# Second raw buffer, later transposes and gated GpSimd work in a fused attention and wave-MLP kernel

## The chip, the cores and the metric

The kernel runs on one core of one Trainium2 chip. Times are device microseconds (us) of one execution. Executions are called fast or slow by their time and their granted TensorE clock (the share of TensorE's full speed that the chip allowed); only fast ones enter a ratio. A difference counts as slower or faster only from 2% on; where a smaller one is called slower, its 95% interval leaves out 1.

## The reference

Windowed attention with four sink positions feeds a "wave" MLP. The cut version:

```python
# q, k, v: (4 batches, 8 heads, 768, 64); n_sink 4, window 128
scores = scale * q @ k^T
keep   = (column < 4) | (0 <= row - column < 128)
a      = softmax(where(keep, scores, -1e9))
x      = (a @ v)                      # heads side by side: (4, 768, 512)
theta  = x @ w_theta
y      = w_tok_r @ (x * cos(theta)) + w_tok_i @ (x * sin(theta))
u      = x + y
out    = u + relu(u @ w_ch)           # float32
```

## The kernel before

Heads are worked on in pairs: four pairs a batch, sixteen "slots" (0 to 15). A slot holds a pair's scores, its exponentials (ScalarE), the mask products (VectorE) and the values of the pair before (slots 11 and 15 do the mask products of two pairs), and a token block of the previous batch's MLP: 12 token-mixing matmuls (`yp`, in four "pieces"), the sum `u`, its transpose `uT`, and four channel matmuls (`wp`). The transposed q and k of pairs 0 to 11 are copied into place by ScalarE or VectorE; those of the last batch (12 to 15) are transposed by DMA straight into the form that the scores read. Pairs 10 and 11 go through a "raw" buffer and a copy. A tile pool with n buffers makes the writer of the n+1st tile wait for the readers of the first.

The program keeps its own order on TensorE, ScalarE, GpSimd and SP from the start, and on VectorE from batch 1 on. So where a line stands in a slot decides what it queues behind.

```python
    vstage = pool("vstage", 4)      # float32 v as loaded
    cast = pool("cast", 2)          # q, k as bf16
    qkt = pool("qkt", 3)            # q, k transposed
    qkr = pool("qkr", 1)            # raw transposes of pairs 10 and 11
    ...
    def pool_copy(out, in_):
        nc.gpsimd.tensor_scalar(out=out, in0=in_, scalar1=1.0, scalar2=1.0, op0=ALU.mult, op1=ALU.mult)

    QK_DMA = range(12, NPAIR)
    QK_RAW = (10, 11)
    V_CAST = range(12, NPAIR)       # v loaded and cast by GpSimd's own DMA

    def load_cast_v(i):
        ...
        nc.gpsimd.dma_start(out=vx[:, :, 0:D], in_=v[b, 2 * hp:2 * hp + 2].rearrange("h (t p) d -> p (h t) d", p=P))

    def transposed_by_dma(i):
        if i in QK_RAW:
            for name in ("q", "k"):
                raw = qkr.tile([P, NT, P], BF16, name=f"{name}r", tag=f"{name}r")
                nc.sync.dma_start_transpose(out=raw, in_=qk_c.pop((name, i))...)
        if i not in QK_DMA:
            return
        for name in ("q", "k"):
            ...
            nc.sync.dma_start_transpose(out=x..., in_=c...)

    def mask_product(i, c):
        E, r = e_t[i], (slice(0, 1024), slice(1024, NE))[c - 1]
        nc.vector.tensor_tensor(out=E[:, :, r], in0=E[:, :, r], in1=mask2[:, :, r], op=ALU.mult)

    def mix(b, t, lo, hi):          # one piece: three of the twelve yp matmuls
        ...
        if hi == 2 * NT:
            ...                     # u = yp + x on VectorE
            if (b, t) not in U_PE:
                nc.sync.dma_start_transpose(out=uT, in_=u)

    def sink_values(b):             # four GpSimd copies
        for tb in range(NB):
            nc.gpsimd.tensor_scalar(out=vsinks[b % 2][:, tb, :, 0:D], in0=vsf[:, b - 2, :, :], ...)

    def slot(i, blk, wtok=None):
        ...
        if i + 2 < HP or HP <= i < NPAIR - 2:
            cast_qk(i + 2)          # GpSimd
        cast_v(i)
        if i + 2 in V_CAST:
            load_cast_v(i + 2)
        ...                         # scores, pieces
        if not first:
            mask_product(i - 1, 1)
            mask_product(i - 1, 2)
        transposed_by_dma(i + 2)
        ...
        if not first:
            piece(blk, 3)           # u and its transpose
        if hp > 0:
            weigh(i - 1, 0)         # values of the pair before
            weigh(i - 1, 1)
        ...
        finish()                    # wp

    # main loop, batches 1 to 3
            if b > 1:
                slot(i, (p, hp))
                if b == 2 and hp == 3:
                    sink_values(3)
    ...
        phases(b, 2)                # the last cos and sin (cs) and products z of the batch
```

The softmax here doesn't subtract the row's maximum and nothing guards it: scores larger than these inputs give would overflow.

## Time and profile before

| kernel before | value |
|---|---|
| median, runs | 183.4 us, 3 runs, 182.77 to 183.54 |
| span of the profiled execution | 180.9 us (device time 182.63 us) |
| mean granted TensorE clock | 0.999 |
| TensorE busy | 169.5 us, 94% |

The lines that carry the argument are shown in the prediction. TensorE is the bound, and its waits are short: 1.6 us from 84 to 145 us. A line of the waits reads "engine, operation and line, <- engine and tile waited for: us in total, times, longest". A line of an engine in order of time reads "start, duration, engine, line, operation, output<-input, count", with the idle time ahead of it in brackets.

One more view is needed for comparison: the mask products "of slots 9 and 11" on VectorE, in the kernel before. Those of slot 9 are pair 9's, which the program does in slot 10; the four of slot 11 are those of pairs 10 and 11.

```profile
91.27 3.00 DVE L247 TENSOR_TENSOR E<-E,mask 128x2048 bf16<-128x2048 bf16 x2
97.38 5.05 DVE L247 TENSOR_TENSOR E<-E,mask 128x2048 bf16<-128x2048 bf16 x4
```

### The profile page before, as it was taken

To read this page: it belongs to the slowest core of one execution; us is meant where nothing else is said; L and a number is where in the kernel's file an instruction comes from. 1 tells how busy PE (TensorE), PEld (TensorE's weight loads), DVE (VectorE), ACT (ScalarE), POOL (GpSimd) and SP (SyncE) were. 2 spreads that over 40 slices of the span, in tenths; PEclk is the share of its full clock that TensorE was granted. 3 is DMA by queue.
4 is the path that set the end of the run, shared out by engine and by line. 5 is a ranking of instruction groups with operands and counts; after the bars stand their busy time and mean duration, and the time that the engine had idled before them with its cause. 6 is when DMAs were issued, how large, how long until landed. Compare 5 with 4: busy or idle time off the path is not lost.

```text
span 180.9 us, 4035 instructions
## 1 busy us (share of the span) xinstructions
PE 169.5 (94%) x1619; PEld 88.4 (49%) x1619; DVE 121.9 (67%) x215; ACT 105.7 (58%) x112; POOL 75.4 (42%) x101
## 2 busy tenths in 40 slices
PE   7799998999999989999998899989999999999991
PEld 2345664554565656443553454434555544344550
DVE  6477867892866688386698981885978816824451
ACT  4897869629768486699998503797454039200000
POOL 8996689987764805038098300750000000000000
PEclk9999999999999999999999999999999999999999
DMA  5999999999998997991399956999733520133413
GB/s 176 307 312 266 350 381 410 383 349 332 328 300 264 287 297 183 282 207 32 102 136 192 220 144 170 297 139 176 118 94 98 147 70 2 59 106 97 145 60 116
DMA packets 73106, 36.80 MB, mean 203 GB/s; under 512 B 61184, under 2 KB 67584, under 8 KB 73088
## 3 DMA queue, kind: packets, MB, share of 16 engines
q1 hardware_dynamic: 65584, 35.60, 71.1%
q0 software_dynamic: 7360, 0.82, 7.3%
q8 instruction: 12, 0.20, 0.5%
q10 hardware_dynamic: 144, 0.13, 0.2%
q14 instruction: 6, 0.05, 0.1%
HBM read 25.82 MB, written 6.29 MB: 178 GB/s over the span
## 4 chain that ended last, share of the span: by engine, by line
PE 64%; ACT 15%; DVE 11%; DMA 3%; issue 3%; POOL 2%; DVEq 0%; ACTq 0%; POOLq 0%
PE yp L372 24%; PE wp L400 9%; PE thp L330 9%; PE avp L277 5%; PE sc L228 5%; ACT E L241 3%; DVE zz L343 3%; ACT cs L339 3%; DVE E L247 3%; ACT cs L340 3%; DMA uT<-u 3%; PE sc L221 2%; PE tp L202 2%; PE wtp L357 2%; PE xtp L307 2%
## 5 line engine op out<-in xcount | busy, mean ns | idle before, releaser
L372 PE MATMUL yp<-zz,wrT 128*128 128x512 bf16 x138 | 52.4, 380 | 1.6 <-DVE zz L343 1.2
L241 ACT ACTIVATE E<-sc 128x1024 bf16<-128x1024 f32 x48 | 47.6, 1032 | 10.6 <-PE sc L228 8.7
L372 PE MATMUL yp<-zz,wiT 128*128 128x512 bf16 x138 | 52.3, 379 | 0.6 <-DVE wiT L361 0.3
L343 DVE TENSOR_TENSOR zz<-cs,x_nat 128x1024 bf16<-128x1024 bf16 x24 | 21.6, 936 | 14.3 <-ACT cs L340 14.3
L247 DVE TENSOR_TENSOR E<-E,mask 128x768 bf16<-128x768 bf16 (+1 forms) x27 | 26.3, 1014 | 1.9 <-ACT E L241 1.9
L76 POOL TENSOR_SCALAR q<-qf 128x768 bf16<-128x768 f32 x14 | 12.3, 881 | 30.6 <-DMA qf<-in_q_dram 15.2
L400 PE MATMUL wp<-wch,uT 128*128 128x512 bf16 x92 | 23.7, 380 | 0.9 <-DMA uT<-u 0.8
L376 DVE TENSOR_TENSOR u<-yp,x_nat 128x512 bf16<-128x512 f32 x23 | 15.9, 690 | 11.0 <-PE yp L372 10.2
L330 PE MATMUL thp<-wth,xT 128*128 128x512 bf16 x96 | 22.8, 379 | 0.1
L339 ACT ACTIVATE cs<-thp,half_pi 128x1024 bf16<-128x1024 f32 (+1 forms) x13 | 13.7, 1051 | 15.5 <-PE thp L330 15.4
L403 DVE SCALAR_TENSOR_TENSOR of<-wp,u 128x512 f32<-128x512 f32 x23 | 15.8, 687 | 9.9 <-PE wp L400 9.8
L372 PEld LDWEIGHTS <-wiT 128*128 128x128 bf16 x138 | 13.5, 98 | 15.3 <-issue 2.4
L372 PEld LDWEIGHTS <-wrT 128*128 128x128 bf16 x138 | 13.5, 98 | 13.5 <-issue 1.7
L277 PEld LDWEIGHTS <-E 128*128 128x128 bf16 x480 | 16.9, 97 | 3.7 <-issue 0.9
L228 PE MATMUL sc<-qT,kT 64*128 64x256 bf16 x192 | 16.6, 264 | 1.4 <-ACT kT L206 0.8
L283 DVE TENSOR_TENSOR x_nat<-avp,rec 128x384 bf16<-128x384 f32 x27 | 15.1, 558 | 0.9
L76 POOL TENSOR_SCALAR k<-kf 128x768 bf16<-128x768 f32 x14 | 14.2, 1015 | 3.1 <-issue 1.2
L228 PEld LDWEIGHTS <-kT 64*128 64x128 bf16 x192 | 6.4, 94 | 16.5 <-issue 12.3
L330 PEld LDWEIGHTS <-xT 128*128 128x128 bf16 x96 | 9.1, 98 | 10.7 <-DVE xT L312 0.6
L277 PE MATMUL avp<-vx,E 128*128 128x65 bf16 x297 | 13.2, 193 | 0.0
L429 ACT COPY lT<-ltp 128x256 bf16<-128x256 bf16 x2 | 0.7, 372 | 21.2 <-PE ltp L427 21.2
L76 POOL TENSOR_SCALAR vx<-vf 128x768 bf16<-128x768 f32 x12 | 12.0, 1005 | 1.9 <-DMA vf<-in_v_dram 1.9
(82 smaller groups left out, 211.6 us busy)
## 6 DMA issues: line engine op xcount, KB each, us to landing
qf<-in_q_dram SPq DMA_DIRECT2D x16, 384.0 KB, 5.5
kf<-in_k_dram SPq DMA_DIRECT2D x16, 384.0 KB, 5.8
out_dram<-of SPq DMA_DIRECT2D x23, 256.0 KB, 2.3
vf<-in_v_dram SPq DMA_DIRECT2D x12, 384.0 KB, 5.3
wf<-in_moe_w_tok_r_dram SPq DMA_DIRECT2D x6, 384.0 KB, 6.6
wf<-in_moe_w_tok_i_dram SPq DMA_DIRECT2D x6, 384.0 KB, 7.6
sqf<-in_moe_w_theta_dram SPq DMA_DIRECT2D x2, 512.0 KB, 6.5
sqf<-in_moe_w_ch_dram SPq DMA_DIRECT2D x2, 512.0 KB, 8.0
```

Source lines behind the costliest of these rows:

```text
L76: nc.gpsimd.tensor_scalar(out=out, in0=in_, scalar1=1.0, scalar2=1.0, op0=ALU.mult, op1=ALU.mult)
L228: nc.tensor.matmul(sc[:, e, 256 * part:256 * part + n], lhsT=kT[r, m * P:(m + 1) * P], rhs=qT[r, m * P:m * P + n], start=not biased, stop= ...
L241: nc.scalar.activation(out=E[:, :, 512 * c:512 * (c + 1)], in_=sc, func=AF.Exp, scale=SCALE)
L247: nc.vector.tensor_tensor(out=E[:, :, r], in0=E[:, :, r], in1=mask2[:, :, r], op=ALU.mult)
L277: nc.tensor.matmul(avp[:, t, :], lhsT=lhsT, rhs=rhs, start=(j == 0), stop=(j == len(seq) - 1), skip_group_check=True)
L330: nc.tensor.matmul(th_t[b, g][:, st, :], lhsT=xT[:, cb, 2 * g + st, :], rhs=wth[:, cb, :], start=(cb == 0), stop=(cb == NC - 1))
L339: nc.scalar.activation(out=cs[:, part, 0, :], in_=thp[:, part, :], func=AF.Sin, bias=half_pi)
L343: nc.vector.tensor_tensor(out=z_t[b][:, 2 * g + st, :, :].rearrange("p o (c n) -> p o c n", c=HP), in0=cs[:, st, :, :].rearrange("p o (c n ...
L372: nc.tensor.matmul(yp, lhsT=wT[i][:, t, sc, :], rhs=z_t[b][:, sc, i, :], start=(j == 0), stop=(j == 2 * NT - 1))
L376: nc.vector.tensor_tensor(out=u.rearrange("p (c n) -> p c n", c=HP), in0=yp.rearrange("p (c n) -> p c n", c=HP), in1=x_t[b][:, :, t, :], o ...
L400: nc.tensor.matmul(wp, lhsT=uT[:, cb, :], rhs=wch[:, cb, :], start=(cb == 0), stop=(cb == NC - 1))
L403: nc.vector.scalar_tensor_tensor(out=of, in0=wp, scalar=0.0, in1=u, op0=ALU.max, op1=ALU.add)
```

## The change

Its intent is to get `u` transposed sooner and to keep GpSimd, which reads the same memory, away from VectorE's products. Raw q and k get two buffers. Loaded v gives one up to pay for them. In slots 10 and 11 the transposes of pairs 12 and 13 go behind `u`. The sink copies, and the casts and v loads of pairs 14 and 15, wait behind one-column copies ("gates") of a tile that VectorE writes. The casts of pairs 14 and 15 thereby leave slots 12 and 13, and their transposes follow `u` of slots 12 and 13 too (`QK_DMA` is 12 to 15).

```diff
-    vstage = pool("vstage", 4)
+    vstage = pool("vstage", 3)
-    qkr = pool("qkr", 1)
+    qkr = pool("qkr", 2)
+    gate = consts.tile([P, 1], BF16)
@@ slot
-        if i + 2 < HP or HP <= i < NPAIR - 2:
+        if i + 2 < HP or HP <= i < NPAIR - 4:
             cast_qk(i + 2)
         cast_v(i)
-        if i + 2 in V_CAST:
+        if i + 2 in V_CAST and i < NPAIR - 4:
             load_cast_v(i + 2)
@@ slot, after the mask products
-        transposed_by_dma(i + 2)
+        if i + 2 not in QK_DMA:
+            transposed_by_dma(i + 2)
@@ slot, after the last piece
             piece(blk, 3)
+        if i + 2 in QK_DMA:
+            transposed_by_dma(i + 2)
         if hp > 0:
@@ main loop
-                if b == 2 and hp == 3:
-                    sink_values(3)
         i = b * HP + HP - 1
+        if b == 2:
+            pool_copy(gate, e_t[i][:, 0, 0:1])
+            sink_values(3)
@@ end of the batch
         phases(b, 2)
+        if b == 2:
+            pool_copy(gate, z_t[b][:, NT - 1, 0, 0:1])
+            for n in (3, 4):
+                cast_qk(i + n)
+            for n in (3, 4):
+                load_cast_v(i + n)
```

## The prediction

> **What bounds the kernel now.** I read the page's busy shares first, then the 40 slices, then TensorE's own order of instructions, the chain of waits, and last the SP queue, because the change moves transfers there. A "slot" below is the program's step for one pair of heads: slots 8 to 11 are batch 2 (about 79.5 to 103 us), slots 12 to 15 batch 3 (116.9 to 140 us). "u" is the 128x512 block that is turned by a DMA transpose into uT before its last matmuls ("wp").
>
> The busy shares and the slices of TensorE and the DMA engines (each digit is tenths of a slice of 4.5 us):
>
> ```profile
> PE 169.5 (94%) x1619; PEld 88.4 (49%) x1619; DVE 121.9 (67%) x215; ACT 105.7 (58%) x112; POOL 75.4 (42%) x101
> PE   7799998999999989999998899989999999999991
> DMA  5999999999998997991399956999733520133413
> ```
>
> TensorE is the bound at 94%; only its holes can be won. The change touches slots 8 to 15, so I summed busy time over stretches: TensorE is busy 4.47 us of 95 to 100, 4.41 of 100 to 105, 4.46 of 115 to 120, and all of 85 to 95, 105 to 115 and 120 to 140. The holes there are 0.53 + 0.59 + 0.54 = 1.66 us, under 1% of the span. TensorE's waits from 84 to 120 us (who waited for whom: total, times, longest) name them:
>
> ```profile
> PE wp L400 <- DMA uT<-u: 0.8, 2, 0.5
> PE yp L372 <- DVE zz L343: 0.5, 1, 0.5
> PE yp L372 <- DVE u L376: 0.3, 1, 0.3
> ```
>
> All three lead elsewhere. The SP queue in order of time (start, duration of the issue) shows why uT is late:
>
> ```profile
> 85.73 0.53 SPq L404 DMA_DIRECT2D out_dram<-of  x1
> 88.04 1.22 SPq L182 DMA_TRANSPOSE qr<-q  x1
> 89.46 1.21 SPq L182 DMA_TRANSPOSE kr<-k  x1
> 90.77 1.22 SPq L382 DMA_TRANSPOSE uT<-u  x1
> ...
> 94.10 1.26 SPq L189 DMA_TRANSPOSE qT<-q  x1
> 95.45 2.21 SPq L189 DMA_TRANSPOSE kT<-k  x1
> 97.76 1.22 SPq L382 DMA_TRANSPOSE uT<-u  x1
> ```
>
> SP stands from 86.26 to 88.04; its wait list has 1.6 us of "qr" waiting for ScalarE's copy out of the single raw buffer. VectorE had written the first u by 89.37, yet its transpose goes out at 90.77, and the second u, written by 94.96, goes out at 97.76, behind q and k of pair 12. VectorE in the same stretch, from the chain of waits:
>
> ```profile
> 90.77 4.88 DMA uT<-u
> 95.65 0.05 issue
> 95.70 1.05 PE wp L400 x4
> 96.75 0.02 issue
> 96.77 0.69 DVE of L403
> 97.47 3.37 DVE E L247 x3
> ```
>
> The four mask products of slot 11 take 5.05 us together; four in slots 13 and 14, beside an idle GpSimd, take 1.68 + 1.68 = 3.36. In the slow four, GpSimd was copying sink values (four copies, 96.85 to 100.89 us).
>
> **What the Trainium skill says.** "SBUF — State Buffer", "Who interferes with whom": VectorE with two SBUF inputs contends with a GpSimd instruction that reads SBUF, the pair is an exclusive lock, and the second one blocks. The trace agrees: 5.05 against 3.36 us for the same four products; z products (both inputs in SBUF) take 1.92 and 2.34 us a pair beside GpSimd's casts at 113 to 118 us, against 1.29 without. "DMA: Bandwidth & Descriptors", "Issuing engines are not separate DMA queues": transfers of SP and GpSimd run on the same engines and interleave. The trace agrees: a q transpose issued at 88.04 beside nothing lands 2.5 us after issue; k of pair 14, issued at 117.81 beside two casting loads of v from GpSimd's queue, lands after 5.0.
>
> **The change part by part.**
>
> (a) A second raw buffer. In slot 9, q and k of pair 11 are issued at 86.3 instead of 88.04; two issues of about 1.35 us later SP is free at 89.0, so u goes at 89.4 and uT lands at 92 to 94, not 95.65. The matmuls that need it can begin at 95.16 (end of the values before them) instead of 95.70: **gain 0.54**.
>
> (b) q and k of pair 12 behind u in slot 10. u goes at 95.0 instead of 97.76, landing at about 98.5, and is wanted at 101. The 0.28 us wait goes.
>
> (c) The copies of sink values wait for a one-column copy from slot 11's E tile. Its last writer in program order, for those columns, is the first mask product of slot 11, so three of the four products run free of GpSimd: 5.05 becomes about 3.4 plus up to one blocked stretch of 0.7 for the fourth. ScalarE's exponentials then set the pace: the third of slot 11 ends at about 100.2, the fourth product at 101.1 (101.6 if blocked), u at 101.8 (102.3), against 103.03. TensorE would be ready at 101.95. Together with (a) and (b) TensorE is ahead by 0.8 to 1.1 there, so (b) and (c) add **0.45** to the 0.54.
>
> (d) Casts of q and k of pairs 14 and 15 move behind the last z of batch 2, so the z products of 113 to 119 us run uncontended. The third pair of ScalarE's cs ends at 118.48; a free VectorE writes the z product that TensorE waits for 0.7 us later, at 119.2 instead of 119.65. TensorE, through before it at 119.15, is itself about 1 us earlier, and so is cs: **gain 0.35** of the 0.54.
>
> (e) The price of (d): q and k of pair 14 were issued at 116.45 and 117.81; now they follow u of slot 12, at about 122.0 and 123.4. Slot 14's first scores come at 128.31 minus about 1.4, so 126.9. Alone k would land at 125.9. But the casts end near 122.6, and GpSimd's v loads follow at once; their data begins about 2 us after issue, at 124.7, into the last three quarters of k's transfer. At half rate, k lands at about 127, at worst 128.4. Expected **loss 0.35**, range 0 to 1.5. Pair 15 has the same distance from u, but the v loads are nearly done, and a stall in 14 gives it slack.
>
> (f) Three buffers for loaded v. The fourth v load, issued at 13.9, must wait for the first v cast, 14.88 to 16.1: a bubble of up to 1 us in a saturated DMA. GpSimd's casts of v, wth and the token weights slide by up to 1 us, but TensorE uses them late: the first wth half is cast at 23.2 and used at 24.63, the last v at 19.6 and used at 23.0, the first token weight at 25.2 and used at 27.12. Hidden; I charge **0.05**. Later v loads find a free buffer (v11, issued at 74.78, needs the cast that ended at 71.96).
>
> Sum: 0.54 + 0.45 + 0.35 - 0.35 - 0.05 = 0.94, about 0.95 us. After slot 15 TensorE is nearly dense to the end, so what is won by then stays: 183.4 - 0.95 = 182.45, taken as **182.4 us**.
>
> **Rivals.** First, the late transposes of pairs 14 and 15 become the bound: k's 5.0 us landing beside v loads, if repeated at 123.4, gives 128.4, a stall of 1.5 us that eats everything and leaves 183.4 to 183.9. For it: GpSimd's loads were taking turns with that very transfer; against: only the tail of k overlaps now. Second, nothing: if TensorE's waits are moved rather than removed (u's write kept late by the blocked fourth product, ScalarE full from 80.8 to 96.9 us and so a floor under slots 9 and 10), only 0.3 us is won, 183.1. Against: ScalarE sat idle waiting for scores from 97 on. Third, the early bubble reaches TensorE and costs 0.5 to 1 us; the slack of 1.4 us and more speaks against it. Fourth, all holes close and no stall comes: 1.6 us, 181.8.
>
> **Range and chances.** The holes cap the gain at 1.66 us, or 0.9%; 2% is 3.7 us, so faster by over 2% is nearly excluded, 0.02. A loss of 3.7 us would need stalls in both late slots and an early loss: 0.03. Same 0.95. The runs of before spread over 0.77 us, so I take 181.3 to 183.6.
>
> **What would show it.** Right: uT in slot 9 issued near 89.4 and no TensorE wait for uT at 90 to 105; the mask products of slot 11 under 4.2 us; z pairs at 1.3 us before the last; GpSimd's four late casts near 118.7 to 122.6. Wrong: a TensorE wait for kT or qT at the start of slot 14 or 15 of over 1 us (step e), a wait for u near 102 that remains (step c), or a TensorE hole at 24 to 40 us beyond the 0.9 us of now (0.4 for zz, 0.3 for wiT, 0.2 for x) (step f).

## The result, and the profile after

The changed kernel takes **188.53 us** (median of four runs, 188.48 to 189.46). The kernel before took 183.47 us beside it (182.77 to 183.73). The ratio is **1.030**, with a 95% interval of 1.0265 to 1.0335: slower. A ratio compares fast runs of the same rounds, so it is not quite the ratio of the medians. The changed kernel's mean clock was 0.976 to 0.991, that of before 0.999 in its profiled execution and 0.991 to 1.0 in the experiments. All outputs are right.

The page of the changed kernel, busy shares and slices:

```profile
PE 171.7 (91%) x1619; PEld 88.8 (47%) x1619; DVE 119.6 (64%) x215; ACT 105.6 (56%) x112; POOL 75.3 (40%) x103
PE   7797998999999999999989999996599999999991
PEclk9999999999999999999999999999799999999999
```

Of the 8s that the prediction wanted to fill (slices 22, 23 and 27 of before), 23 is still one, and slice 21 has become one. One new hole stands in slices 28 and 29 (about 127 to 136 us), and in the second of these the granted clock falls too.

TensorE's waits from 84 to 145 us, changed kernel:

```profile
PE sc L228 <- DMA kT<-k: 3.9, 1, 3.9
PE avp L277 <- DVE E L247: 0.5, 1, 0.5
PE wp L400 <- DMA uT<-u: 0.5, 1, 0.5
PE sc L228 <- ACT E L241: 0.3, 1, 0.3
```

The three waits of before have changed place or gone, and one wait of 3.9 us, for k of pair 14, is more than all of them. GpSimd and the SP queue in order of time, changed kernel, show where k came from:

```profile
121.59 0.19 POOL L76 TENSOR_SCALAR gate<-zz 128x1 bf16<-128x1 bf16 x1 [15.53 <-DVE zz L343]
121.74 0.83 POOL L76 TENSOR_SCALAR q<-qf 128x768 bf16<-128x768 f32 x1
...
124.13 0.83 POOL L76 TENSOR_SCALAR k<-kf 128x768 bf16<-128x768 f32 x1
124.91 2.08 POOL L148 DMA_DIRECT2D vx<-in_v_dram  x2
```

```profile
123.31 1.20 SPq L382 DMA_TRANSPOSE uT<-u  x1
124.61 1.23 SPq L189 DMA_TRANSPOSE qT<-q  x1
125.94 1.30 SPq L189 DMA_TRANSPOSE kT<-k  x1
```

Both v loads were issued one us before k's transpose. The chain of work that ended last, same kernel (start, duration, what):

```profile
125.94 7.46 DMA kT<-k
133.40 0.05 issue
133.44 0.61 PE sc L228 x4
134.05 2.67 PE yp L372 x6
...
137.44 1.40 PE yp L372 x6
```

The transpose takes 7.46 us to land. TensorE was ready at 129.56 us, so it waits 3.88 us. Then six `yp` matmuls take 2.67 us, where the same six take 1.40 us a little later. The stretches show why; the columns are the busy us of PE, weight loads, DVE, ACT and POOL, then clock, DMA share and GB/s:

```profile
130.00:132.00 2.00, 0.00 (x0) 0.00 (x0) 2.00 (x3) 0.00 (x0) 0.00 (x0) 1.00 2.04 136
132.00:134.00 2.00, 0.56 (x5) 0.15 (x6) 0.09 (x1) 0.00 (x0) 0.00 (x0) 0.84 1.98 230
134.00:136.00 2.00, 2.00 (x7) 0.72 (x6) 0.00 (x0) 1.02 (x1) 0.00 (x0) 0.50 1.00 202
136.00:138.00 2.00, 2.00 (x21) 0.74 (x20) 0.00 (x0) 0.86 (x1) 0.00 (x0) 0.80 0.82 224
```

The clock is 0.50 from 134 to 136 us: TensorE is fully busy, but with 7 matmuls in 2 us. The Trainium skill, "TensorE: Matmul & The Clock Gate", section "HAM oscillation — how this bites in real kernels", gives the rule "no PE-idle gaps >~3.4µs", else the clock drops to half. The trace agrees: the idle gap of 3.88 us was followed by 0.50.

VectorE in the changed kernel shows what the gates did:

```profile
93.02 3.81 DVE L247 TENSOR_TENSOR E<-E,mask 128x2048 bf16<-128x2048 bf16 x2
99.33 1.69 DVE L247 TENSOR_TENSOR E<-E,mask 128x2048 bf16<-128x2048 bf16 x2
101.63 1.70 DVE L247 TENSOR_TENSOR E<-E,mask 128x2048 bf16<-128x2048 bf16 x2 [0.61 <-ACT E L241]
```

The four products of slot 11 fell from 5.05 to 1.69 + 1.70 = 3.39 us. The two of slot 9 rose from 3.00 to 3.81 us. GpSimd's casts for slot 11 (q, k, v) ran beside them in both kernels (91.25 to 94.97 us before, 93.01 to 96.42 us after); what differs is who was held. Before, the first product took 1.91 us and the cast of k 1.77; after, the product took 2.71 us and the cast of k 0.84. The two products took 3.00 or 3.01 us in all four traces with one raw buffer and no gate on these casts, and 3.80 or 3.81 in all eight with two. Why the turn goes the other way is not shown.

**Where the time went.** The start times of the same matmuls in both traces, after minus before, split the 6.8 us between the two profiled spans (180.9 and 187.7):

| TensorE matmul | before | after | difference |
|---|---|---|---|
| first theta sum (batch 0) | 24.63 | 26.40 | +1.77 |
| first `yp` after slot 11 | 103.08 | 103.98 | +0.90 |
| channel sums of slot 12 | 121.75 | 122.94 | +1.19 |
| first scores of slot 14 | 128.31 | 133.44 | +5.13 |
| channel sums of slot 14 | 132.94 | 139.61 | +6.67 |

So 0.6 us were won in the middle, 3.9 lost in front of slot 14 and 1.5 to the low clock behind it. The +1.77 at the start is treated with care: the profiled execution of after was 0.9 us slower than its median, that of before 0.8 us faster, and the medians differ by 5.1 us, not 6.8.

### The profile page after: what moved, and what is told of

The parts are those of the page before. It is cut to its first block, busy times and chain, and to the rows that moved or that the text cites. A ratio compares the mean times of both kernels' runs of the same rounds, so it can differ in the third digit from the quotient of the medians.

```text
span 187.7 us, 4027 instructions
## 1 busy us (share of the span) xinstructions
PE 171.7 (91%) x1619; PEld 88.8 (47%) x1619; DVE 119.6 (64%) x215; ACT 105.6 (56%) x112; POOL 75.3 (40%) x103
## 4 chain that ended last, share of the span: by engine, by line
PE 56%; DMA 12%; ACT 12%; DVE 10%; SPq 3%; issue 2%; POOL 2%; POOLq 0%; DVEq 0%; ACTq 0%
PE yp L372 21%; PE thp L330 9%; PE wp L400 8%; DMA vf<-in_v_dram 6%; PE avp L277 5%; DMA kT<-k 4%; DVE E L247 4%; PE sc L228 4%; DMA uT<-u 3%; SPq L119 3%; ACT cs L339 3%; ACT cs L340 3%; ACT E L241 3%; DVE zz L343 2%; PE wtp L357 2%
## 5 line engine op out<-in xcount | busy, mean ns | idle before, releaser
L372 PE MATMUL yp<-zz,wrT 128*128 128x512 bf16 x138 | 53.2, 385 | 1.0 <-DVE zz L343 0.6
L372 PE MATMUL yp<-zz,wiT 128*128 128x512 bf16 x138 | 53.1, 385 | 0.3 <-ACT wiT L359 0.2
L343 DVE TENSOR_TENSOR zz<-cs,x_nat 128x1024 bf16<-128x1024 bf16 x24 | 19.3, 843 | 16.7 <-ACT cs L340 16.5
L76 POOL TENSOR_SCALAR q<-qf 128x768 bf16<-128x768 f32 x14 | 13.2, 940 | 16.5 <-PE tp L202 10.1
L76 POOL TENSOR_SCALAR k<-kf 128x768 bf16<-128x768 f32 x14 | 13.4, 956 | 4.0 <-PE sc L228 1.3
```

Of the source, the lines that this page charges most:

```text
L343: nc.vector.tensor_tensor(out=z_t[b][:, 2 * g + st, :, :].rearrange("p o (c n) -> p o c n", c=HP), in0=cs[:, st, :, :].rearrange("p o (c n ...
L372: nc.tensor.matmul(yp, lhsT=wT[i][:, t, sc, :], rhs=z_t[b][:, sc, i, :], start=(j == 0), stop=(j == 2 * NT - 1))
```

## The experiments

**Theory L**: the late transposes of pair 14 meet the v loads, k lands after TensorE needs it, and the clock falls. **Rival S**: the start (three v buffers, or the moved addresses behind the new 32-byte tile) costs it. **Rival M**: the middle (raw buffers, order) costs it by disturbing VectorE. Each ratio below is against the kernel before. Some edits take raw tiles from the pool `wraw`, already there with four buffers for the token weights, since four v buffers and two raw buffers do not fit the on-chip memory together.

### One part alone: three v buffers

```diff
-    vstage = pool("vstage", 4)
+    vstage = pool("vstage", 3)      # in the kernel before
```

> The kernel before with three buffers for loaded v and nothing else. Theory S (the start pays for the missing buffer): as in the changed kernel's trace, TensorE's first values wait about 1 us for the first v cast and everything from 24 us on is 1.8 us later: 185.2 us (184.7 to 185.7). Rival N (the 1.8 us at the start is a difference between two executions): 183.4 us, within 0.4 of before.

Measured: 182.56 us, ratio 0.9993 (0.9916 to 1.0071); first theta matmul at 24.77 us against 24.63. The third buffer costs nothing that shows: this half of rival S falls.

### The change with four v buffers

```diff
-    vstage = pool("vstage", 3)
+    vstage = pool("vstage", 4)
-    qkr = pool("qkr", 2)
-                raw = qkr.tile([P, NT, P], BF16, name=f"{name}r", tag=f"{name}r")
+                raw = wraw.tile([P, NT, P], BF16, name=f"{name}r", tag="raw")
```

> The changed kernel with four buffers for loaded v again; the raw q and k of pairs 10 and 11 take the four buffers of the raw token weights, which are idle by then, so that it fits. Theory S: the start of before comes back, 188.5 - 1.8 = 186.7 us; the hole at the start of slot 14 stays at 3 to 4 us. Rival N: 188.5 us.

Measured: 189.24 us, ratio 1.0336 (1.0278 to 1.0394). Giving the buffer back repairs nothing. TensorE's wait for k is even longer, the landing of k 8.4 us, and the clock again 0.50 from 134 to 136 us:

```profile
PE sc L227 <- DMA kT<-k: 4.9, 1, 4.9
```

### The change with its v loads early

```diff
             sink_values(3)
+            load_cast_v(14)
 ...
             thetas(b, 0)
+            if b == 2:
+                pool_copy(gate, z_t[b][:, 1, 0, 0:1])
+                load_cast_v(15)
             finish()
 ...
-            for n in (3, 4):
-                load_cast_v(i + n)      # at the end of the batch
```

> The changed kernel, but the casting loads of v for pairs 14 and 15 go out early (14 behind the sink copies at about 106, 15 behind the first z at about 117), so that no load of GpSimd's queue runs beside the transposes of k and q of pairs 14 and 15. Theory O (the overlap of these loads with the transposes makes the 3.9 us hole and the lower clock after it): k of pair 14, issued near 126, lands 2.5 us later, before slot 14; no hole and no lower clock: 183.2 us (182.7 to 184.2). Rival P (issue behind u and behind the casts is late enough by itself): the hole stays above 2 us, 186 us or more.

Measured: 185.44 us, ratio 1.0150 (1.0077 to 1.0222). With the casts as late as in the change but the loads gone from beside k, k lands in 3.8 us, the wait for k is 0.26 us, and the clock stays at 1.00. That is theory L's first half. It misses the expected time because the early load made a wait of its own: 2.00 us at 111.44 us, TensorE waiting for a transpose of x that was issued at 105.77 us, 1.2 us behind the load. TensorE's waits from 84 to 145 us:

```profile
PE thp L330 <- DMA xT<-x_nat: 2.0, 1, 2.0
PE avp L277 <- DVE E L247: 0.5, 1, 0.5
PE sc L228 <- DMA kT<-k: 0.3, 1, 0.3
```

### The change without its last gate

```diff
-        if i + 2 < HP or HP <= i < NPAIR - 4:
+        if i + 2 < HP or HP <= i < NPAIR - 2:
             cast_qk(i + 2)
-        if i + 2 in V_CAST and i < NPAIR - 4:
+        if i + 2 in V_CAST:
 ...
-        if b == 2:                       # gate, casts and loads of 14 and 15
-            pool_copy(gate, z_t[b][:, NT - 1, 0, 0:1])
-            ...
```

> The changed kernel with casts and v loads of pairs 14 and 15 back in slots 12 and 13; the transposes of all four last pairs stay behind u. Theory O: the v loads are done by about 126 as in the kernel before, so k of pair 14 lands within 3 us and the hole is below 1 us: 184 us (183.3 to 184.8), with z products slowed by GpSimd again (0.3 to 0.5 us). Rival P: a hole of over 2 us at slot 14, 186 us or more.

Measured: 183.98 us, ratio 1.0061 (0.9999 to 1.0122). The transposes of pairs 14 and 15 are still behind `u` (k of 14 issued at 124.95 us), but the loads go out at 116.71 and 120.32 us. TensorE's wait for k is now:

```profile
PE sc L228 <- DMA kT<-k: 0.7, 1, 0.7
```

The ratio falls from 1.030 to 1.006 by undoing this one part: 0.024 of 183 us, about 4.4 of the 5.1 us, lie in it. A wait of 0.7 us is left, with the last transposes still behind `u`.

### Only the v loads late

```diff
         phases(b, 2)
+        if b == 2:
+            for n in (3, 4):
+                cast_qk(i + n)          # not gated: as early as in the version above
+            pool_copy(gate, z_t[b][:, NT - 1, 0, 0:1])
+            for n in (3, 4):
+                load_cast_v(i + n)
```

> The run with the early casts, but GpSimd's two v loads of pairs 14 and 15 are held behind the last z as in the changed kernel, so that of the late pieces only the loads are late. Theory O (the overlap of these loads with the transposes of q and k of pair 14 makes the hole): the casts done, q and k of pair 14 still go out behind u at about 124.5 to 126, the loads' data follow at about 124 to 127, and the hole at slot 14 grows from 0.7 to 2 us or more[...]: 186 to 188.5 us. Rival C (the late casts made the hole): 0.7 us hole, 184 us.

Measured: 186.07 us, ratio 1.0144 (1.0105 to 1.0183), landing of k 5.9 us. TensorE's waits, and the stretches of the same kernel:

```profile
PE sc L228 <- DMA kT<-k: 2.0, 1, 2.0
```

```profile
130.00:132.00 2.00, 0.27 (x4) 0.11 (x4) 2.00 (x3) 0.00 (x0) 0.00 (x0) 1.00 0.72 206
132.00:134.00 2.00, 2.00 (x26) 0.87 (x22) 0.08 (x1) 1.13 (x2) 0.00 (x0) 1.00 1.23 185
134.00:136.00 2.00, 2.00 (x35) 1.22 (x34) 0.37 (x1) 1.83 (x2) 0.00 (x0) 1.00 0.90 202
```

Making the loads late takes the version above from 1.006 to 1.014 of before (the two intervals overlap) and lengthens its wait from 0.7 to 2.0 us. That is not the whole of the 3.9: without the four casts (0.8 us each) in front of them the loads go out at 122.02 us, 3.75 us ahead of k rather than 1.03. An idle gap of 2.0 us, and the clock stays at 1.00 with 26 and 35 matmuls in a stretch where the changed kernel did 5 and 7. So the changed kernel pays twice: a longer gap, and a clock drop that a gap of 2 us did not bring.

### The new tile's 32 bytes

```diff
+    gate = consts.tile([P, 1], BF16)     # in the kernel before, unused
```

> The kernel before plus an unused one-column tile at the place of the changed kernel's gate tile: every later buffer in SBUF lies 32 bytes further on, nothing else differs. Theory A (the 32 bytes, not the missing v buffer, slow the loads at the start): the first v cast begins near 16 us instead of 14.8, the first theta matmul near 25.5 instead of 24.7, and the time is 0.8 to 1.8 us above before: 184.0 to 185.2 us. Rival N (the start differs from execution to execution): first v cast near 14.8, time within 0.4 us of before.

```diff
-    gate = consts.tile([P, 1], BF16)     # in the change; the gates write junk instead
-            pool_copy(gate, ...)
+            pool_copy(junk, ...)
```

> The changed kernel with its gate copies written to a one-column tile that is already there, so that the 32 bytes go and all else stays. Theory A: the start of before comes back (first v cast near 14.8 us, first theta matmul near 24.7), 1 to 1.8 us less than the changed kernel: 187.0 us (186.7 to 187.7). Rival N: 188.5 us, first v cast anywhere from 14.8 to 17. In both, the hole at slot 14 stays at 3 to 5 us with a lower clock after it.

Measured: 183.11 us, ratio 1.0010 (0.9961 to 1.0060), and 188.69 us, ratio 1.0297 (1.0253 to 1.0341). The tile is not the cause: before stays where it was with it, the change stays slow without it (wait for k 3.64 us, clock down to 0.50). With both halves gone, rival S is out. Something of it stays open. The first cast of v began at 14.8 to 15.2 us in ten traces without the tile and at 15.9 to 17.1 in six with it, but at 16.38 in this last one, which is without it too. The time of the kernel before did not follow it (first cast at 16.72 us with the unused tile, ratio 1.0010).

### Raw buffers and order alone, then the sinks, then the casts

Three steps up from the kernel before. First the raw buffers from `wraw` and pairs 12 and 13 behind `u`:

```diff
-        transposed_by_dma(i + 2)
+        if i + 2 not in (12, 13):
+            transposed_by_dma(i + 2)
 ...
             piece(blk, 3)
+        if i + 2 in (12, 13):
+            transposed_by_dma(i + 2)
```

> The kernel before with two parts of the change alone: raw q and k of pairs 10 and 11 in separate buffers (those of the raw token weights, so that four v buffers stay and nothing moves in SBUF), and q and k of pairs 12 and 13 behind u. Theory G (the steps of the prediction for uT hold): no wait for uT between 90 and 105 us, 0.5 to 0.9 us faster than before: 182.7 us. Rival M (the wait moves to the mask products, as the 0.54 us wait for the mask at 96.9 in the changed kernel suggests): within 0.3 us of before.

Then, on top, the gate of the sinks:

```diff
                 if b == 2 and hp == 3:
+                    pool_copy(junk, e_t[i][:, 0, 0:1])
                     sink_values(3)
```

> As the run with the raw buffers and the order alone, plus the sink copies held behind the first mask product of slot 11 (the gate writes to a one-column tile that is already there). Theory G: the four mask products of slot 11 take 3.4 us instead of 5.0 and the wait for u near 102 us goes: 0.3 to 0.5 us less than without it, 1 us less than before: 182.3 us. Rival: no further gain, because ScalarE's exponentials set that stretch.

Then, on top, a gate that the change has not: the casts for slot 11 wait for the mask products of slot 9.

```diff
+        if i == 11:
+            pool_copy(junk, e_t[9][:, 0, 1024:1025])
         if i + 2 < HP or HP <= i < NPAIR - 2:
             cast_qk(i + 2)
```

> The run with raw buffers, order and sinks, plus GpSimd's casts of q, k and v for slot 11 held behind the last mask product of slot 9. Theory L (the port that VectorE and GpSimd share makes the 0.5 us wait for the mask near 95): the two mask products of slot 9 take 1.7 us instead of 3.8, that wait goes, 0.5 us less than that run (183.96): 183.4 us. Rival: another wait takes its place, no change.

Measured: 185.68 us, ratio 1.0143 (1.0095 to 1.0192); then 183.96 us, 1.0050 (1.0007 to 1.0092); then 183.21 us, 1.0003 (0.9960 to 1.0046). Parts (a) and (b) alone make the kernel slower by 1.4%, which neither expectation allowed; the second version also missed its 182.3 us, the third came as expected. In the first of the three, TensorE's waits and VectorE's mask products:

```profile
PE yp L371 <- DVE zz L342: 1.4, 2, 0.8
PE yp L371 <- DVE u L375: 1.0, 1, 1.0
PE avp L276 <- DVE E L246: 0.5, 1, 0.5
```

```profile
91.08 3.80 DVE L246 TENSOR_TENSOR E<-E,mask 128x2048 bf16<-128x2048 bf16 x2
97.39 5.55 DVE L246 TENSOR_TENSOR E<-E,mask 128x2048 bf16<-128x2048 bf16 x4
```

Both waits for `uT` are gone, as intended, and longer ones for VectorE stand in their place: 2.9 us for `z`, `u` and the masked E, against 0.8 us before for `z` and `u`. All waits of this trace add up to 1.5 us more than those of before, in its fastest execution; the medians differ by 2.9 us, so part of the loss stays unexplained. Rival M is real, but it is not the loss of the change, whose own gates take much of it away again. The sinks gate brings slot 11 to 1.69 + 1.69 us, and the casts gate slot 9 to 1.68 us; with it the wait for the masked E is gone.

### Building the version that the traces point to

The traces ask for the same parts with the v loads gated behind the *first* z instead of the last, so that they are done before k needs the DMA engines, and with the casts gate of the previous run:

```diff
+            if b == 2:                       # after thetas(b, 0)
+                pool_copy(junk, z_t[b][:, 1, 0, 0:1])
+                load_cast_v(14)
+                load_cast_v(15)
 ...
+        if b == 2:                           # after phases(b, 2)
+            pool_copy(junk, z_t[b][:, NT - 1, 0, 0:1])
+            for n in (3, 4):
+                cast_qk(i + n)
```

All four pairs are transposed behind `u` here.

> All of the change's intent with the faults taken out: raw buffers without moving SBUF, all four transposes behind u, sinks and casts of slot 11 gated, casts of pairs 14 and 15 behind the last z, but their v loads issued right behind the first z (about 116), so that their data is done before the transposes begin near 123. Theory O: no hole at slot 14 above 0.5 us although casts and transposes are late, no waits for z, u or the mask above 0.3 us: 181.9 us (181.3 to 182.6), 0.5% below before. Rival P (late casts and transposes are the fault): a hole of over 2 us, 185 us.

The same with one raw buffer and pairs 12 and 13 ahead of `u`, as before:

> The same gates and load times as the run before it in this list, but the single raw buffer and the old order of q and k of pairs 12 and 13 (ahead of u). Tells what the second raw buffer and the order are worth once GpSimd no longer blocks VectorE: by the prediction's steps a and b 0.5 to 0.8 us more than that run, 182.6 us; if they are worth nothing, the same as that run.

Measured: 182.38 us (181.6 to 184.24), ratio 0.9956 (0.9910 to 1.0003), and 182.96 us, ratio 0.9986 (0.9937 to 1.0035). In the first, v is loaded from 114.61 us on, k of pair 14 lands in 4.1 us, and TensorE's waits from 84 to 145 us are short. The two differ by 0.6 us, as was expected of the second raw buffer and the order, but their intervals overlap. The waits of the first:

```profile
PE wp L399 <- DMA uT<-u: 0.8, 1, 0.8
PE sc L227 <- DMA kT<-k: 0.5, 1, 0.5
```

Then, in the first, the last two pairs ahead of `u` as in the kernel before, to tell whether the queue's order behind `u` still costs:

```diff
-        if i + 2 not in (12, 13, 14, 15):
+        if i + 2 not in (12, 13):
             transposed_by_dma(i + 2)
 ...
-        if i + 2 in (12, 13, 14, 15):
+        if i + 2 in (12, 13):
             transposed_by_dma(i + 2)
```

> The run with all gates and the v loads behind the first z, but q and k of pairs 14 and 15 go ahead of u again (12 and 13 stay behind u). Theory B (the 0.5 us hole that is left at slot 14 is the place behind u, with the v loads out of the way): k of pair 14 is issued near 121.2 instead of 123.2, no hole at slot 14, 0.4 to 0.5 us less: 181.9 us, 0.9% below before. Rival: u's transpose, now behind q and k, becomes late for slot 13, and the time stays at 182.4.

Measured: 182.59 us, ratio 0.9973 (0.9921 to 1.0026). k lands in 2.5 us and no wait for it is left, but `uT` pays:

```profile
PE wp L399 <- DMA uT<-u: 1.9, 2, 1.1
```

Last, one more `u` block turned by TensorE instead of by DMA, and the kernel before once more, as a check:

```diff
-    U_PE = {... (1, 3), (1, NT - 1), ...}
+    U_PE = {... (1, 3), (1, NT - 2), (1, NT - 1), ...}
```

> As the run before it in this list, and u of the fifth block of batch 1 is transposed by TensorE (0.34 us of TensorE, 0.4 us of VectorE) instead of by DMA, whose landing TensorE awaited 0.4 to 0.8 us near 110 us in every run with the second raw buffer. Expected: that wait goes, 0.3 us less: 181.6 us; rival: the copy by VectorE delays the next blocks and nothing is gained.

> The kernel before, unchanged, traced once more. Rival N of the first runs (the start differs from execution to execution): the first v cast lies anywhere from 14.8 to 17 us in this trace too, away from 14.88; if it is again within 0.2 us of 14.88 the start of the changed kernel is a matter of the kernel.

Measured: 182.62 us (181.09 to 184.26, with one slow run that the ratio leaves out), ratio 0.9978 (0.9906 to 1.0050), and 182.75 us for the kernel before again (one run, state unknown; the four others of the call 182.27 to 183.05), its first v cast at 14.77 us. The first one's profiled execution has a span of 179.1 us, the shortest of all, and no wait of TensorE over 0.3 us from 84 to 175 us. Over its runs that is no gain that shows. No version clearly beats the kernel before; the best interval just touches 1.

### What k's landing hung on

Issue times from the traces, for pair 14:

| kernel | v loads issued | kT issued | loads ahead of kT | kT landed after |
|---|---|---|---|---|
| change, four v buffers | 124.16 (both) | 125.21 | 1.05 | 8.4 |
| change | 124.91 (both) | 125.94 | 1.03 | 7.5 |
| change without the tile | 123.47 (both) | 124.52 | 1.05 | 7.2 |
| raw buffers and order alone | 116.53 and 119.20 | 119.77 | 3.24 and 0.57 | 6.3 |
| only the v loads late | 122.02 (both) | 125.77 | 3.75 | 5.9 |
| before | 115.93 and 119.05 | 117.81 | 1.88 and -1.24 | 5.0 |
| gates, old order | 115.23 (both) | 124.21 | 8.98 | 4.5 |
| change without its last gate | 116.71 and 120.32 | 124.95 | 8.24 and 4.63 | 4.2 |
| gates, v loads at first z | 114.61 (both) | 123.16 | 8.55 | 4.1 |
| change, v loads early | 104.58 and 118.22 | 126.20 | 21.6 and 7.98 | 3.8 |
| gates, last pairs ahead of u | 115.05 (both) | 121.62 | 6.57 | 2.5 |

Five more traces with the loads and transposes placed as before have k landing after 4.9 to 5.1 us. Two groups of costs stand out: a landing of 3.8 to 4.5 us behind `u` with the loads over, and about 3 to 4 us more with both loads issued one us ahead. What makes the place behind `u` slow is not shown: with the last pairs ahead of `u` it is `uT`, issued third, that lands after 4.5 us, but in the version with one more `u` turned by TensorE `uT` in the same place lands after 2.5. The DMA view of the changed kernel from 126 to 134 us (40 cells of 0.2 us: busy share of the DMA engines in tenths and GB/s; then GpSimd's and SP's queues: packets, MB, time of the packets as a share of 16 engines) shows the latter:

```profile
DMA  9998089999999999901112999999999999999998
GB/s 216 214 206 161 18 54 115 103 177 134 106 145 148 144 127 79 22 3 10 10 10 26 195 210 169 163 147 129 147 168 217 211 204 253 339 313 334 266 122 37
q0 software_dynamic: 3104, 0.39, 96.3%
q1 hardware_dynamic: 2145, 0.75, 81.7%
```

The two loads are 3104 packets for 0.39 MB, and those packets' time is 96.3% of 16 engines over these 8 us. With SP's 81.7% that is more than 100%, so packets' times overlap and are not all work. From 129.2 to 130.4 us hardly anything moves though both queues have work outstanding, and from 129.4 on in this stretch the engines' busy share is 0 to 2 tenths. What stops them there no run tells; stretches of 7 to 19 GB/s appear also where the loads are over, as in the change without its last gate.

## Why the prediction was wrong

The time was predicted as 182.4 us within 181.3 to 183.6, and measured as 188.53. By its steps:

- **(a)** and **(b)**: right in what they removed, wrong in what they were worth. TensorE waits for no `uT` from 90 to 105 us. But the mask products of slot 9 were held by GpSimd's casts for longer (3.00 to 3.81 us), and TensorE waits 0.54 us for the masked E at 96.89 us, as much as (a) was to win; a wait of 0.47 for `uT` appears at 112.84 us. Alone, the two parts lost 1.4%.
- **(c)**: right. Predicted at 3.4 us for the four products with up to 0.7 for a blocked one, measured at 3.39.
- **(d)**: right. The z pairs run at 1.29 us each and TensorE waits for none of them. (a) to (d) together were to win 1.34 us; the start times show 0.6.
- **(e)** is **the step that failed**. "At half rate, k lands at about 127, at worst 128.4" allowed 3.6 us, at worst 5.0, from an issue at 123.4. The order of events was right. All of it came about 2.5 us later, with k at 125.94, the loads one us ahead of it, and TensorE ready at 129.56, 3.6 us after the issue, as planned (126.9 against 123.4). Only the landing, 7.46 us, was twice what was allowed. The trace of before had shown 5.0 us beside two loads issued 3.1 us apart, one ahead of k and one behind it, and nothing of both issued at once right ahead; to take that 5.0 for the worst case was the mistake. It was not even the worst of that trace: k of pair 12, issued at 95.45 us with one v load issued at 95.72, landed after 6.0 us. The case without loads was too short as well: behind `u` with the loads over k took 3.8 to 4.5 us, not 2.5, and TensorE waited 0.26 to 0.93 us for it. The term was sized at 0.35 us, range 0 to 1.5, and measured as 3.9 us of waiting.
- **The clock** was in no step. A stall was priced at its own length. The gaps of 3.64, 3.88 and 4.86 us were all followed by half clock, 1.5 us more in the trace of the change and longer in the version without the tile, at 0.50 from 132 to 136 us; the two gaps of 2.0 us were not. The page cited above states the rule, and I had not drawn on it.
- **(f)**: right. Three v buffers alone gave 0.9993.
- The first **rival** was the right one by mechanism. It was sized by a landing of 5.0 us, giving 1.5 us of stall.

The cause of the loss is shown by undoing it (1.030 to 1.006), by moving the loads alone away from k (wait 3.9 to 0.26 us) and by making the loads alone late (0.7 to 2.0 us). That the rest of the 3.9 us comes of the loads going out only one us ahead of k is read from the table and not from a run that changes this alone. Two more things stay open: where the last 0.6% of the version without the gate lies, if it is more than noise (its interval begins at 0.9999), and why versions with nearly no TensorE wait are not measurably faster than before.

## What to carry to other kernels

When a load or a transpose is moved later to free an engine, draw up the DMA engines' own calendar at the new place: a transfer that TensorE waits for should not follow casting loads that were issued just ahead of it, and its landing time is to be measured there rather than carried over from another place. Price a TensorE stall with the clock drop that follows it once it is as long as those of 3.64 us and more here, so that 3.9 us of waiting becomes 5.4; no run shows where between 2.0 and 3.64 us the drop begins. A gate costs one small copy and does keep GpSimd away from VectorE's products (5.05 to 3.39 us here), but the work that it holds back lands on something else, so the gate's release has to be chosen with the next consumer in view, as with the first z instead of the last.

## What the Trainium skill lacked or had wrong

- "DMA: Bandwidth & Descriptors", section "🔬 Queues, rings and completion order", says that each DMA engine takes turns between the queue rows packet by packet. It gives no cost for a transpose beside casting loads. Here k's transpose landed after 2.5 us ahead of `u` with no load beside it, after 3.8 to 4.5 behind `u`, and after 7.2 to 8.4 with two casting loads issued one us ahead. Taking turns is not all of it: in the trace of the change there is a stretch of 3 to 26 GB/s, about one us long, in which most engines were idle while both queues had work.
- The same page says that a casting transfer has to be issued by GpSimd, but not what it costs the engines: two of 192 KB were 3104 packets, whose times, overlapping with those of the other queue, added up to 96.3% of 16 engines over 8 us.
- "SBUF — State Buffer", section "Who interferes with whom", describes the lock between VectorE and GpSimd and names slowdowns of 6.8 and 1.5 times by issue order, but gives no figure for products like these: the same pair of mask products took 1.68 us free of GpSimd, and 3.00 or 3.81 us beside the same three casts, depending on whether the cast of k or the product was held.
- "TensorE: Matmul & The Clock Gate" had it right: gaps of 3.64, 3.88 and 4.86 us brought clock 0.50, two of 2.0 us did not.
